# Moving 256 KB of one weight load from partitions 64-127 to partitions 0-63, and so from eight DMA engines to the other eight, in a decode kernel that streams 170 MB

## The chip, the cores and the metric

One core of one Trainium2 chip. The metric is the device time of one execution in microseconds (us), median over runs. The kernel of before took 402.03 us (401.67 to 402.33, four runs beside those of the change). All timed runs named here lie within 1.5% of the fastest run of the same kernel and count as fast.

## The reference

Two branches of a decode step for one token are added: attention over a KV cache of 65536 positions with 4 KV heads, and a small MLP "mixer". Cut to what matters:

```python
xn = layernorm(x)
# A: q = xn @ wq; softmax(q k^T) v over 65536 positions; @ wo       (the 128 MB of K and V)
# B: with S = 1 the shifted groups of h are all padding, so hs is 0 @ w2
h  = gelu(layernorm(xn) @ w1)
hs = concat(shifted quarters of h) @ w2      # w2: 1024 x 1024 bf16, 2 MB
x1 = xn + hs
h2 = gelu(layernorm(x1) @ w3) @ w4           # w3: 1024 x 3584, w4: 3584 x 1024
out = x + A + (x1 + h2)
```

The kernel still loads w2 and multiplies it, with a vector of zeros (`g_bf`). The layout of w2 in memory can therefore not change the result.

## The kernel before

All large loads are issued on one queue, in the order wq, w1, w2, w3, then K and V blocks of 8 MB (k0, v0, k1, ...), wo, and w4 in four parts. Three slots of SBUF take turns; a load is issued when its slot has been read.

```python
def rows_src(w, r0, nrow):          # partition p gets rows p*r .. p*r+r-1
    return w.rearrange("(p r) n -> p (r n)", p=P)[:, r0 * w.shape[1]:(r0 + nrow) * w.shape[1]]
kv_load(0, "s0", rows_src(A_wq, 0, 8), 8 * HQD)
kv_load(1, "w1", rows_src(B_w1, 0, 8), 8 * D, b_w1)
_dma(q_sp, chan("w2"), lambda e: e.dma_start(out=KV[:, 1, 8 * D:16 * D], in_=rows_src(B_w2, 0, 8)), writes=b_w2)
kv_load(2, "s2", rows_src(B_w3, 0, 8), 8 * F)
# ... (cut)
def proj(s, o, ncol, vec, bank, reads, c0):
    # ... for each of 8 rows j of a partition, and each column group k:
    mv = bass.AP(KV[:].tensor, s * SLOT + o + j * ncol + 4 * k, [[kvstep, P], [nper, P], [1, 4]])
    e.matmul(S_ps[...], vec[:, j:j + 1].broadcast_to([P, 32]), mv, start=(j == 0), stop=(j == KT_D - 1), ...)
# ... (cut)
proj(1, 0, D, xn2_bf, 2, b_w1 + [b_xn2], 256)
proj(1, 8 * D, D, g_bf, 3, b_w2 + [b_const], 272)     # w2 times zeros
issue(4)                                              # v0 goes into the slot of w1 and w2
# ... (cut; at the end of the kernel:)
w4_parts = [(0, 17), (17, 7), (24, 3), (27, 1)]       # rows a partition; four loads
# ... matmuls of a part start when it has landed; then one copy and the output
def Ttr(n, idx):                                      # VectorE transposes, 1024 columns each
    for ix in idx: _op(q_dve, lambda e, o=o: e.transpose(...))
```

## Time and profile before

| Reading | Value | Where it stands |
|---|---|---|
| Busy share of TensorE, VectorE | 44%, 56% | engines of the page |
| Loads' queue, share of 16 DMA engines' span | 98.4% | DMA queues |
| Last landing of w4's last load | 397.79 of 400.7 us | completion marks |
| Distance of first to last engine in that load | 3.19 us | completion marks |

Lines of the page of the kernel before: busy time of the engines, and, for 40 equal slices of the span, the granted TensorE clock in tenths, the busy share of the DMA engines in tenths and what they moved; then packets and queues.

```profile
PE 176.5 (44%) x1611; PEld 70.7 (18%) x1627; DVE 224.5 (56%) x347; ACT 25.2 (6%) x53; POOL 7.1 (2%) x30
...
PEclk9999668556655655555556656555566656555588
DMA  9999899999999999999999999999999999999994
GB/s 419 419 391 486 381 478 445 420 425 419 432 419 446 464 420 425 419 445 419 440 458 420 419 419 458 427 433 445 428 419 419 446 445 414 445 440 432 393 417 195
...
q1 hardware_dynamic: 3608, 169.87, 98.4%
q8 instruction: 13, 0.21, 0.2%
q14 instruction: 5, 0.04, 0.0%
```

The DMA engines are at least 80% busy in every slice but the last, so the kernel is bound by its loads. Two small queues carry instructions, 18 transfers in all.

The end of the chain of waits of the kernel before (start, duration, what):

```profile
369.51 0.33 SPq L534
369.84 0.05 issue
369.89 0.43 SPq L534
370.31 0.05 issue
370.37 26.78 DMA KV<-in_B_w_dram
397.14 0.04 issue
397.18 0.84 PE S_ps L543 x12
398.02 0.14 issue
398.16 0.41 PE S_ps L543 x4
398.57 0.02 issue
398.59 0.43 DVE orow L612
```

The kernel ends with a wait for parts of w4 and, in this chain, 1.9 us of work after it (397.14 to 399.02 us).

A share of busy time can't show which of 16 engines is last. The trace can: a load over 128 partitions leaves 16 completion marks. They are taken as one for each engine: the changed kernel's first load over eight partitions leaves one mark at its issue (3.27 us) and eight at its end (30.36 to 30.72 us). Here are some loads of the kernel before: time of the first mark in us of the span, then all 16 in ns after the first, sorted. (This is worked out from the trace; it is not a view of the profile.)

```
w2       31.27  0 56 67 77 88 102 112 185 195 218 244 254 264 325 393 607
k0       67.59  0 46 59 77 90 103 117 193 245 258 272 317 385 599 1179 1727
block   261.30  0 80 187 240 247 293 534 780 1473 1509 1518 1610 1660 1667 1809 2044
block   319.34  0 105 165 171 529 603 708 1529 1546 1565 1646 1697 1706 1786 1855 3052
w4 last 394.60  0 109 163 176 521 581 680 1690 1771 1807 1846 3038 3067 3083 3104 3186
```

All 16 engines move the same bytes, as far as the packets show (128, 256 or 2304 of each large size, multiples of 16, and w2's marks within 0.61 us of each other), but some fall behind in steps. The steps come from the instruction transfers: before a 16384 B one begins, its engine's marks are in the first group, after it they are 1.5 us later; a lone engine is pushed by the 8192 B ones at 60, 189 and 314 us, about 1.0 us each. (The other two 8192 B ones, at 261 and 285 us, hit other engines.) DMA records of the kernel before around the first 16 KB one (queue, start and end in ns of the span, duration, bytes):

```
1 47874 50300 2426 65536      (another engine, for comparison)
8 47899 48925 1026 16384      (instructions)
1 48920 51881 2961 65536      (the next packet of the engine that carried them)
```

That engine's packet ends at 51.88 instead of about 50.33 us: 1.55 us lost. By the end five engines are 3.0 to 3.2 us late, four 1.7 to 1.85.

### The profile page before, as it was taken

The numbers are of one execution on the slowest core, as the hardware profiler recorded it, in microseconds if no ns is written. First come the engines' busy times: TensorE is split into PE (matmuls) and PEld (weight loads), VectorE is DVE, ScalarE is ACT, GpSimd is POOL, SyncE is SP. The second block draws the span as 40 slices with busy tenths as digits, with TensorE's granted clock in tenths as the row PEclk, the third lists the DMA queues.
The fourth block names the chain that finished last, engine by engine and source line by source line (L and its number), as shares of the span: only waits on it lengthen the run. The fifth ranks groups of instructions, "written<-read, shape, count | busy, mean of one in ns | idle before, by whom it ended". The sixth has DMA issues, their size and how long they took to land.

```text
span 400.7 us, 3966 instructions
## 1 busy us (share of the span) xinstructions
PE 176.5 (44%) x1611; PEld 70.7 (18%) x1627; DVE 224.5 (56%) x347; ACT 25.2 (6%) x53; POOL 7.1 (2%) x30
## 2 busy tenths in 40 slices
PE   0034767245334513374345342643462335437664
PEld 0022435011011101121111120111121111102242
DVE  0024221985398446763985558659746685696400
ACT  1000000011001100101011001100110011010100
POOL 5000000000000000000000000000000000000000
PEclk9999668556655655555556656555566656555588
DMA  9999899999999999999999999999999999999994
GB/s 419 419 391 486 381 478 445 420 425 419 432 419 446 464 420 425 419 445 419 440 458 420 419 419 458 427 433 445 428 419 419 446 445 414 445 440 432 393 417 195
DMA packets 3770, 170.13 MB, mean 425 GB/s; under 512 B 548, under 2 KB 552, under 8 KB 808
## 3 DMA queue, kind: packets, MB, share of 16 engines
q1 hardware_dynamic: 3608, 169.87, 98.4%
q8 instruction: 13, 0.21, 0.2%
q14 instruction: 5, 0.04, 0.0%
q10 hardware_dynamic: 144, 0.00, 0.0%
HBM read 169.87 MB, written 0.00 MB: 424 GB/s over the span
## 4 chain that ended last, share of the span: by engine, by line
DMA 41%; DVE 30%; PE 23%; issue 3%; another core or an unknown queue 2%; POOL 0%; SPq 0%; ACT 0%; DVEq 0%
DMA KV<-in_A_k_cache_dram 29%; DVE KV L436 21%; PE S_ps L448 8%; DMA KV<-in_B_w_dram 7%; DMA KV<-in_A_x_dram 6%; PE OT_ps L492 5%; PE S_ps L385 3%; DVE pT_f L483 2%; PE M_ps L400 2%; DVE mrow L455 2%; PE S_ps L353 1%; PE M_ps L520 1%; DVE Yall L369 1%; PE PT_ps L479 1%
## 5 line engine op out<-in xcount | busy, mean ns | idle before, releaser
L436 DVE STREAM_TRANSPOSE KV<-KV 128x1024 f32<-128x1024 f32 x128 | 148.6, 1210 | 8.8 <-DMA KV<-in_A_k_cache_dram 8.7
L448 PE MATMUL S_ps<-KV,Yall 128*32 128x512 bf16 x512 | 60.7, 622 | 114.5 <-DVE KV L436 114.5
L492 PE MATMUL OT_ps<-KV,pT_f 128*32 128x512 bf16 x512 | 59.3, 612 | 1.3 <-PE OT_ps L492 1.3
L448 PEld LDWEIGHTS S_ps<-KV,Yall 128*32 128x32 bf16 x512 | 16.8, 125 | 148.0 <-DVE KV L436 132.2
L483 DVE STREAM_TRANSPOSE pT_f<-PT_ps 128x512 f32<-128x512 f32 x32 | 22.6, 706 | 28.2 <-PE S_ps L448 12.0
L470 ACT ACTIVATE p_sb<-S_ps,brun 128x1024 bf16<-128x1024 f32 x16 | 17.8, 1115 | 281.0 <-DVE brun L468 177.3
L455 DVE TENSOR_REDUCE mrow<-S_ps 128x1 f32<-128x1024 f32 x16 | 19.5, 1216 | 16.8 <-PE S_ps L448 16.7
L479 PE MATMUL PT_ps<-p_sb,permR 128*128 128x512 bf16 x16 | 8.8, 553 | 37.2 <-DVE pT_f L483 37.2
L492 PEld LDWEIGHTS OT_ps<-KV,pT_f 128*32 128x32 bf16 x512 | 17.1, 132 | 35.0 <-issue 33.3
L505 DVE SCALAR_TENSOR_TENSOR O_acc<-O_acc,ff,OT_ps 128x512 f32<-128x512 f32 x12 | 8.9, 744 | 23.6 <-PE OT_ps L492 23.6
L385 PE MATMUL S_ps<-KV 128*32 128x512 bf16 x88 | 12.3, 549 | 2.9 <-DVE KV L333 2.9
L458 PE MATMUL M_ps<-Rm,Lmat 128*128 128x16 bf16 x16 | 3.1, 192 | 22.6 <-DVE Rm L456 22.5
L313 DVE CAST KV<-KV 128x8 f32<-128x8 bf16 x1 | 0.2, 171 | 22.3 <-DMA KV<-in_A_x_dram 22.3
L479 PEld LDWEIGHTS PT_ps<-p_sb,permR 128*128 128x128 bf16 x32 | 3.3, 102 | 43.1 <-ACT p_sb L470 15.4
L612 DVE CAST orow<-S_ps 128x256 bf16<-128x256 f32 x1 | 0.4, 426 | 15.8 <-PE S_ps L543 15.8
L400 PE MATMUL M_ps<-ident_f,pT_f 64*128 64x2 f32 (+2 forms) x32 | 7.9, 373 | 2.3 <-DVE pT_f L393 2.3
L400 PEld LDWEIGHTS M_ps<-ident_f,pT_f 64*128 64x128 f32 (+2 forms) x32 | 7.7, 326 | 4.3 <-DVE pT_f L393 4.3
L393 DVE COPY pT_f<-S_ps 64x512 f32<-64x512 f32 (+1 forms) x3 | 2.1, 686 | 11.1 <-PE S_ps L385 11.1
L523 DVE TENSOR_TENSOR cb_R<-M_ps,maskD 32x128 f32<-32x128 f32 x4 | 1.1, 287 | 12.1 <-PE M_ps L520 12.1
L458 PEld LDWEIGHTS M_ps<-Rm,Lmat 128*128 128x128 bf16 x16 | 1.6, 102 | 34.5 <-DVE Rm L456 34.5
L338 PE MATMUL M_ps<-KV 8*128 8x8 bf16 x1 | 0.2, 161 | 16.2 <-DVE Dmat_f L337 16.2
L543 PE MATMUL S_ps<-KV,gh_bf 128*1 128x256 bf16 x112 | 4.2, 290 | 6.1 <-DMA KV<-in_B_w_dram 5.9
(82 smaller groups left out, 95.4 us busy)
## 6 DMA issues: line engine op xcount, KB each, us to landing
KV<-in_B_w_dram SPq DMA_DIRECT2D x1, 7168.0 KB, 48.1
KV<-in_B_w_dram SPq DMA_DIRECT2D x1, 4352.0 KB, 21.5
KV<-in_B_w_dram SPq DMA_DIRECT2D x2, 2048.0 KB, 28.3
KV<-in_B_w_dram SPq DMA_DIRECT2D x1, 1792.0 KB, 25.4
KV<-in_B_w_dram SPq DMA_DIRECT2D x1, 768.0 KB, 26.8
KV<-in_B_w_dram SPq DMA_DIRECT2D x1, 256.0 KB, 27.0
KV<-in_A_k_cache_dram SPq DMA_DIRECT2D x8, 38.9
KV<-in_A_v_cache_dram SPq DMA_DIRECT2D x8, 29.8
```

The lines of the kernel that those rows point to most:

```text
L385: fns.append(lambda e, j=j, k=k, mv=mv: e.matmul(S_ps[32 * (k % 4):32 * (k % 4) + 32, bank + k // 4, :], vec[:, j:j + 1].broadcast_to([P, ...
L400: fns.append(lambda e, b=b, nb=nb, c=c: e.matmul(M_ps[:, c0 + 16 * b + c:c0 + 16 * b + 4 * nb:4], pT_f[0:32 * nb, b, c:512:4], ident_f[0:3 ...
L436: _op(q_dve, lambda e, o=o: e.transpose(out=KV32[:, s, o:o + 1024], in_=KV32[:, s, o:o + 1024]), reads=[b_KV[s][4 * sub + ix]], writes=[b_ ...
L448: fns.append(lambda e, we=we, cm=cm, mv=mv: e.matmul(S_ps[32 * cm:32 * cm + 32, n % 4, :], Yall[:, h, we, :, :].rearrange("p a g -> p (a g ...
L455: _op(q_dve, lambda e: e.reduce_max(mrow[:, k:k + 1], S_ps[:, 2 * k:2 * k + 2, :].rearrange("p b c -> p (b c)"), axis=AX.X), reads=b_S[2 * ...
L458: _op(q_pe, lambda e: e.matmul(M_ps[:, 0:16], Lmat[:, :], Rm[:, k, :], start=True, stop=True), reads=[b_R[k], b_const], writes=[b_M])
L470: _op(q_act, lambda e: e.activation(p_sb[:, :, :].rearrange("p b c -> p (b c)"), S_ps[:, 2 * k:2 * k + 2, :].rearrange("p b c -> p (b c)") ...
L479: _op(q_pe, lambda e: e.matmul(PT_ps[:, :], permR[:, :], p_sb[:, n % 2, :], start=True, stop=True), reads=[b_p[n % 2], b_const], writes=[b ...
L483: _op(q_dve, lambda e: e.transpose(out=pT_f[:, n % 2, :], in_=PT_ps[:, :]), reads=[b_PT], writes=[b_pT[n % 2]])
L492: fns.append(lambda e, q=q, q4=q4: e.matmul(OT_ps[32 * q4:32 * q4 + 32, g % 2, :], pT_bf[:, n % 2, q, :, 1], KV[:, s, 8192 * sub + 512 * q ...
L505: _op(q_dve, lambda e: e.scalar_tensor_tensor(out=O_acc[:, 0:512], in0=O_acc[:, 0:512], scalar=ff[:, k:k + 1], in1=OT_ps[:, k, :], op0=ALU ...
L543: fns.append(lambda e, lhs=lhs, rhs=rhs, jj=jj: e.matmul(S_ps[32 * jj:32 * jj + 1, 0, 0:256], lhs, rhs[:, 256 * jj:256 * jj + 256], start= ...
```

## The change

w2 gets six rows on every partition by the old kind of load, and four more on partitions 0-63 by eight loads, each to eight partitions four apart. This takes 256 KB from partitions 64-127 and gives it to 0-63. In the trace after the change w3's marks stand in two groups of eight, 2.4 us apart: at the 2.42 us of a 64 KB packet that is 64 KB between them, 32 KB less for each of eight engines and 32 KB more for each of the other eight (an estimate from these two numbers). The intent is taken to be balance: the late engines would be those that lose bytes.

No record names an engine, and which engine writes which partitions of a load over 128 partitions no trace here shows. "Low" engines are here the eight that carry the loads over eight partitions, "high" ones the other eight. The recorded texts use the words in this sense, and their "half" is often one of these groups; their "lowest" and their ordinal numbers are an order that the second run of dummy loads gives (w3's marks there: one engine with one step, one with two, and so on up to two with seven, which count as the lowest).

```diff
-        _dma(q_sp, chan("w2"), lambda e: e.dma_start(out=KV[:, 1, 8 * D:16 * D], in_=rows_src(B_w2, 0, 8)), writes=b_w2)
+        NLO = 4
+        NALL = KT_D - NLO // 2
+        b_w2x = [_B() for _ in range(8)]
+        _dma(q_sp, chan("w2"), lambda e: e.dma_start(out=KV[:, 1, 8 * D:(8 + NALL) * D], in_=B_w2[0:P * NALL, :].rearrange("(p r) n -> p (r n)", p=P)), writes=b_w2)
+        for i in range(8):
+            hf, c = divmod(i, 4)
+            p0 = 32 * hf + c
+            src = bass.AP(B_w2.tensor, B_w2.offset + (P * NALL + p0 * NLO) * D, [[4 * NLO * D, 8], [1, NLO * D]])
+            _dma(q_sp, chan("w2%d" % i), lambda e, p0=p0, src=src: e.dma_start(out=KV[p0:32 * (p0 // 32) + 32:4, 1, (8 + NALL) * D:(8 + NALL + NLO) * D], in_=src), writes=[b_w2x[i]])
 ...
-        proj(1, 8 * D, D, g_bf, 3, b_w2 + [b_const], 272)
+        proj(1, 8 * D, D, g_bf, 3, b_w2 + b_w2x + [b_const], 272, NLO)
```

(`proj` runs 10 rows j instead of 8, the last four with 64 partitions, so 20 matmuls instead of 16; `g_bf` is twice as long.)

## The prediction

> **What bounds the kernel now.** In the page's slices the 16 DMA engines are 90% or more busy nearly throughout; the loads' queue has 98.4% of their span. TensorE (44%) and VectorE (56%) have slack. The chain of waits ends in a DMA wait for w4 and about 1.5 us of matmuls and copy. So the DMA engine that finishes its bytes last sets the time. All engines move the same bytes, but don't finish together: the completion marks of w2's load (16 per load) spread over 0.61 us, those of w4's last load over 3.19 us: seven engines within 0.7 us of the first, four 1.7-1.85 us late, five 3.0-3.2 us late.

> **Why.** The DMA records show 13 instruction transfers of 16384 B; each holds its engine for about 1.05 us and lengthens the next 64 KB packet from 2.42 to about 2.9 us: about 1.5 us. Following packets back to back, I find eight engines served in turn: four late ones have two, four have one. One more engine, outside these eight, takes three 8192 B instruction transfers (60, 189, 314 us) at about 1 us each and is 3 us late too. [...]

> **What the change does.** [...] Each low engine then gets 32 KB more and each high engine 32 KB less: at the traced 27.07 B/ns, +1.2 us (1.3 with smaller packets) and -1.2 us. [...] It adds four matmuls (16 took 3.4 us, so 0.85 us) and eight waits on PE in the w2 stage, and eight DMA issues (0.3-0.7 us each, under 6 us) on a queue that still has the 22 us wq load ahead. Both are hidden: v0's issue at 52 us has some 16 us before the engines run dry, k1's at 70 us likewise. w2 meets a zero vector; the result can't change.

> **On the critical path.** Only the balance. If the eight instruction engines are one half, the fifth late engine is in the other: whichever half is loaded, one engine of the +3 us class gets +1.2 us and the kernel ends later. [...] So I expect a slight loss: 403.2 us, range 401.2 to 404.3. Faster by over 2%: 0.01; within 2%: 0.98; slower by over 2%: 0.01.

> **What would show it.** Right: the spread of completion marks in w4's last load grows from 3.2 to about 4.4 us, with one or a few lone latest engines; w4's last landing about 1 us later; DMA busy unchanged in the middle; w2's 20 matmuls in about 4.2 us; k0, k1 issued about 1 us later with no idle DMA slice. Wrong: spread shrinking to about 2 us and a time near 401.

> **What would make it wrong.** [...] instruction transfers placed differently in timed runs; extra instructions bringing another transfer; eight small loads leaving an engine gap; 0.1% noise drowning it.

Passages that rested on a rule which no trace here shows are cut from it, among them which engines write which partitions. Its sum was 402.0 + 1.2 = 403.2 us: one engine of the +3 us class gets 32 KB more, 1.2 us at 27.07 B/ns. That low engines gain 32 KB and high ones lose it was a premise then; w3's marks, 2.4 us apart after the change, show it. Cut with them are two estimates on the other side of the forecast: a gain of 1.2 us if all five late engines lost bytes, and of 0.3 us if some of the +1.7 us class got them. They are no terms of the 403.2.

## The result, and the profile after

The changed kernel takes 402.82 us (402.67 to 403.12, four runs), against 402.03 us for the kernel before: a ratio of 1.0021, 95% interval 1.0004 to 1.0038. Ratios here and below are the mean time of one kernel's fast runs over that of the other's of the same rounds, so not quite the ratio of the medians quoted. It is the same within 2%, and about 0.8 us slower. All outputs are right. Run again for the experiments it was 402.87 against 402.13 us, ratio 1.0021, interval 1.0008 to 1.0033.

The same lines of the page, after:

```profile
PE 186.5 (46%) x1631; PEld 70.7 (18%) x1631; DVE 224.4 (56%) x347; ACT 25.2 (6%) x53; POOL 7.1 (2%) x30
...
PEclk9998657555755565656555556555555556655897
DMA  9999999999999999999999999999999999999994
...
q1 hardware_dynamic: 3736, 169.87, 98.3%
q8 instruction: 13, 0.21, 0.2%
q14 instruction: 5, 0.04, 0.0%
```

The bytes are the same, the DMA engines are as busy as before, and the number of instruction transfers is unchanged. The end of the chain of waits, after:

```profile
370.66 0.33 SPq L544
370.99 0.05 issue
371.04 0.44 SPq L544
371.48 0.05 issue
371.53 0.49 SPq L544
372.02 0.04 issue
372.06 26.84 DMA KV<-in_B_w_dram
398.89 0.06 issue
398.95 0.31 PE S_ps L553 x4
399.26 0.02 issue
399.28 0.42 DVE orow L622
```

The wait for w4 now ends at 398.89 us, with its last part, instead of 397.14 us with the part before the last one. The completion marks, after (as above):

```
w3       47.12  0 27 83 104 207 284 346 433 2402 2467 2524 2533 2541 2549 2569 2758
k0       66.48  0 74 104 197 275 335 432 1558 2402 2466 2524 2537 2550 2564 2758 3549
block   182.70  0 28 208 275 1477 1491 1668 1921 2341 2406 2463 2476 2490 2503 2697 3479
block   202.12  0 218 796 1421 1441 1597 1611 1865 2285 2349 2406 2417 2424 2431 2641 4403
block   240.83  0 787 1430 1450 1596 1620 1759 1873 2284 2350 2397 2417 2431 2444 2640 4402
block   260.19  0 794 1450 1474 1597 1620 1769 1874 2294 2350 2416 2430 2437 3133 4191 4413
block   280.05  0 383 925 954 1110 1125 1273 1377 1797 1862 1910 1934 1943 2636 3685 3906
block   299.38  0 363 951 971 1137 1151 1300 1405 1937 1951 1965 2563 2654 3362 3711 3925
block   318.74  0 374 960 971 1127 1151 1299 1394 1937 1951 1962 2573 2663 3372 3712 4903
w4 last 394.48  0 401 660 803 1432 1464 1481 2015 2032 2067 2157 2209 2467 2871 3223 4410
```

The change labels the engines. In w3 there are two groups of eight, 2.4 us apart: the low eight took 32 KB more, the high eight 32 KB less, 1.2 us each way as intended. Now the steps can be followed:

- The 16 KB transfer at 51.5 us hits a high engine (27 becomes 1558 in k0). So do the next five, judged by which group loses a member.
- The 8 KB transfers at 61, 191 and 317 us hit one and the same low engine. It is last in every load from k0 on (3549, then 4403, then 4903).
- The seventh 16 KB transfer, at 259.9 us, hits a low engine (2640 becomes 4191). So does the eighth, at 291.0 us (1797 becomes 3362, while the eight high marks keep their places); the ninth hits a high one again.
- The two other 8 KB transfers, at 250 and 286 us, hit two other low engines, by about 0.7 us each (3133 and 2563 are new).

So the change unloaded engines that were late, but gave 32 KB more to a low engine that was 3 us late as well. That one engine ends alone, 1.2 us behind the next, and w4's last load lands at 398.89 instead of 397.79 us.

The time grew less (0.8 us) than the landing (1.1 us). Part of this is the tail. Last matmuls of the kernel before, then of the changed one (timeline; start, duration, group):

```profile
397.18 0.81 PE L543 MATMUL S_ps<-KV,gh_bf 128*1 128x256 bf16 x12 [0.96 <-DMA KV<-in_B_w_dram]
398.16 0.38 PE L543 MATMUL S_ps<-KV,gh_bf 128*1 128x256 bf16 x4 [0.16 <-PE S_ps L543]
```

```profile
398.29 0.50 PE L553 MATMUL S_ps<-KV,gh_bf 128*1 128x256 bf16 x12 [0.95 <-DMA KV<-in_B_w_dram]
398.95 0.29 PE L553 MATMUL S_ps<-KV,gh_bf 128*1 128x256 bf16 x4 [0.16 <-DMA KV<-in_B_w_dram]
```

In the profiled run of before, twelve matmuls took 0.81 us and the last four had to wait for them although their data had landed; in the profiled run of after they took 0.50 us. The clock records of the traces show why: 0.5 of full speed from 396.76 us on in the profiled run of before, 1.0 from 395.68 to 399.09 us in that of after. For this pair the sum closes: the landing is 1.10 us later, the tail from landing to the end of the last copy 0.42 us shorter (0.81 instead of 1.23), and the profiled run took 402.67 instead of 401.99 us, 0.68 more. The tail differs from run to run (time of the profiled run less last landing: 3.8 to 4.3 us in all of those whose landing is given here; the twelve matmuls took 0.81 or 0.50 us in all whose end was read).

### The profile page after: what moved, and what is told of

Its sections match the earlier page's. It is cut to its first block, busy times and chain, and to the rows that moved or that the text cites. A ratio compares the mean times of both kernels' runs of the same rounds, so it can differ in the third digit from the quotient of the medians.

```text
span 401.4 us, 4002 instructions
## 1 busy us (share of the span) xinstructions
PE 186.5 (46%) x1631; PEld 70.7 (18%) x1631; DVE 224.4 (56%) x347; ACT 25.2 (6%) x53; POOL 7.1 (2%) x30
## 4 chain that ended last, share of the span: by engine, by line
DVE 36%; DMA 32%; PE 26%; issue 3%; ACT 2%; POOL 0%; SPq 0%; ACTq 0%; DVEq 0%
DVE KV L446 25%; DMA KV<-in_A_k_cache_dram 20%; PE S_ps L458 9%; DMA KV<-in_B_w_dram 7%; PE OT_ps L502 6%; DMA KV<-in_A_x_dram 5%; PE S_ps L395 3%; DVE pT_f L493 3%; DVE mrow L465 2%; PE PT_ps L489 2%; PE M_ps L410 2%; PE S_ps L361 2%; ACT p_sb L480 2%; PE M_ps L530 1%; DVE Yall L377 1%
## 5 line engine op out<-in xcount | busy, mean ns | idle before, releaser
L489 PE MATMUL PT_ps<-p_sb,permR 128*128 128x512 bf16 x32 | 17.8, 556 | 29.1 <-ACT p_sb L480 14.7
L395 PE MATMUL S_ps<-KV 128*32 128x512 bf16 (+1 forms) x92 | 13.0, 551 | 2.9 <-DVE KV L341 2.9
L553 PE MATMUL S_ps<-KV,gh_bf 128*1 128x256 bf16 x112 | 5.4, 355 | 7.0 <-DMA KV<-in_B_w_dram 7.0
```

The source lines that it names most:

```text
L395: fns.append(lambda e, j=j, k=k, mv=mv, pp=pp: e.matmul(S_ps[32 * (k % 4):32 * (k % 4) + 32, bank + k // 4, :], vec[0:pp, j:j + 1].broadca ...
L489: _op(q_pe, lambda e: e.matmul(PT_ps[:, :], permR[:, :], p_sb[:, n % 2, :], start=True, stop=True), reads=[b_p[n % 2], b_const], writes=[b ...
L553: fns.append(lambda e, lhs=lhs, rhs=rhs, jj=jj: e.matmul(S_ps[32 * jj:32 * jj + 1, 0, 0:256], lhs, rhs[:, 256 * jj:256 * jj + 256], start= ...
```

## The experiments

Theory (last engine): the kernel ends when the DMA engine with the most bytes and instruction transfers ends; the change added 1.2 us to such an engine, and its own instructions cost nothing. Rival (extra work): the four matmuls, the eight waits and the eight small loads cost the 0.8 us.

### The change again, as a partner for the others

> The changed kernel again, beside the others on one chip. Last-engine theory: 0.6 to 1.2 us slower than before (ratio 1.0015 to 1.003), spread of the 16 completion marks of w4's last load about 4.4 us against 3.2 us before, with one lone mark last. Extra-work theory (four matmuls, eight waits, eight small loads cost the time): the same total, so this run alone does not tell.

402.87 against 402.13 us, ratio 1.0021 (1.0008 to 1.0033). The last landing is again 398.89 us, spread 4.24 us, with one lone mark last, 1.2 us after the next. It repeats.

### Balanced bytes, all of the extra work (a flawed control)

```diff
-            src = ... [[4 * NLO * D, 8], [1, NLO * D]]      # eight partitions x four rows
+            src = ... [[16 * D, 16], [1, 2 * D]]            # sixteen partitions x two rows
-            out=KV[p0:32 * (p0 // 32) + 32:4, ...]
+            out=KV[i:P:8, ...]
```

> All added instructions of the change kept (20 matmuls on w2, eight waits, eight small loads), but each small load goes to 16 partitions with two rows, so that every engine again gets the same bytes. Last-engine theory: back to the time of before within 0.3 us (ratio 0.999 to 1.0008), spread in w4's last load about 3.2 us with five marks in the last class. Extra-work theory: stays 0.7 us or more slower than before (ratio 1.0015 or more).

It took 403.27 us, ratio 1.0028 (1.0014 to 1.0041): slower than the changed kernel, where the theory expected the time of before. The spread of the marks did go back (3.41 us, five marks in the last class), but all engines were late together: the first mark of w4's last load came at 395.85 us instead of 394.60. The small packets explain it: the 4096 B packets took 267 ns in the median and 159 at least, a mean of 255, and w3's packets 2172 ns in the mean instead of 2118. Eight of each per engine make 8 x 96 + 8 x 54 = 1200 ns, an estimate from these means, against 1250 ns observed. Why packets to these partitions (every eighth) were slower is not shown. The run is no test of the rival. It shows that the way in which the loads are cut can cost more than the change itself.

### The extra rows on partitions 64-127

```diff
-            p0 = 32 * hf + c
+            p0 = 64 + 32 * hf + c
```

(with the source and the matmuls moved to match)

> The extra rows go to partitions 64-127 instead of 0-63, still by loads of eight rows. If a load of eight rows runs on the lowest eight engines whatever partitions it writes: as the changed kernel, w4's last landing near 398.9 us of the span, one lone mark last at about 4.4 us. If the engine follows the partition: the high eight engines get the extra 32 KB, the low eight lose it, four marks (those with two 16 KB instruction transfers) last, the spread about 5 to 5.5 us (3.05 + 1.2 over low engines that are now 1.2 us earlier), the time likewise about 1.2 us over before. Extra-work theory: as the changed kernel in both.

It took 405.85 us, ratio 1.0091 (1.0077 to 1.0104), more than either side expected. The marks settle which engines did it: in w3 again eight are late by 2.26 us or more, and the engine with the three 8 KB instruction transfers is among the eight, while the first 16 KB one hits the other eight, as in the changed kernel. So, as far as these marks tell, the loads over eight partitions ran on the same eight engines for partitions 64-127 as for 0-63. But the first mark of w3 came at 49.80 us instead of 47.12: the high engines lost time too. The 8192 B packets took 643 ns in the median; in the changed kernel, where they go to partitions 0-63, they took 309.

### Dummy loads over 2 to 8 rows

```diff
+        for k in range(2, 9):
+            p0 = k * (k - 1) // 2                     # second run: (0, 1, 2, 3, 32, 33, 34)[k - 2]
+            src = bass.AP(B_w2.tensor, B_w2.offset, [[32 * D, k], [1, 16 * D]])
+            _dma(... out=KV[p0:p0 + k, 1, 16 * D:32 * D] ...)   # second run: every fourth partition
```

> Kernel before plus seven dummy loads over 2, 3, ... 8 rows of 32 KB each (1.21 us per engine). If a load over k rows runs on the lowest k engines: in w3's completion marks, eight engines without a step, and one each later by 1.2, 2.4, 3.6, 4.8, 6.0, 7.2 us and two by 8.5 us, beside the base spread of 0.6 us. The instruction transfers of 16 KB then should all fall on the eight without a step, and the lone engine with three 8 KB ones on one of the steps, which tells its number. Total about 8.5 us longer, more if the lone engine is a low number (up to 11).

418.63 us (one run). Eight marks of w3 stayed together and eight moved, but by 4.0, 4.6, 5.1, 5.4, 7.6, 8.0, 8.9 and 11.3 us: the 32 KB packets took 2.36 us in the median instead of 1.21. The steps can't be read. These loads write neighbouring partitions; that this made them slow was a guess. So I ran it again with every fourth partition:

> Dummy loads over 2, 3, ... 8 rows again, now to every fourth partition, so that each should write at full rate (1.21 us for 32 KB). In w3's completion marks: eight without a step; eight at about 1.2, 2.4, 3.6, 4.8, 6.0, 7.3 and twice 8.5 us. The engine with three 8 KB instruction transfers (the first near 62 us) is the one whose mark moves about 1 us later from w3 to the next load, or that is already 1 us off its step if its w3 mark comes after that: the step tells its number among the low eight.

408.17 us (one run). The 32 KB packets took 1.21 us, and the marks now are a ladder:

```
w3  48.33  0 39 85 131 141 151 200 210 1346 2363 3566 4792 6109 7665 8403 8814
k0  67.68  0 48 85 124 137 151 205 218 1356 3566 3924 4792 7087 7674 8393 8814
```

A load over k rows ran on k engines, among them all those of the smaller loads: one engine with one step, one with two, and so on. Between the two loads 6109 became 7087 and 2363 became 3924. The engine five steps up (the fourth from the ladder's end) took the 8 KB transfer at 61 us; the engine two steps up (the seventh from the end) took the 16 KB one at 52.6 us. So the engines of the 16 KB transfers are not one half of the sixteen: this one is low, and the changed kernel shows two low ones. The second surprise is that here a low one was hit by the first of the thirteen transfers, in the changed kernel none before the seventh.

### The extra work alone, and the matmuls alone

```diff
 # work only: kernel before, w2 whole, plus eight loads of 512 B a row and four repeated matmuls
+            src = bass.AP(B_w2.tensor, B_w2.offset + p0 * 4 * D, [[16 * D, 8], [1, 256]])
-        proj(1, 8 * D, D, g_bf, 3, b_w2 + [b_const], 272)
+        proj(1, 8 * D, D, g_bf, 3, b_w2 + b_w2x + [b_const], 272, 2)
 # matmuls only: no small loads, no further waits
+        proj(1, 8 * D, D, g_bf, 3, b_w2 + [b_const], 272, 2)
```

> Kernel before with the change's extra work and without its shift: w2 stays at eight rows on all partitions, four matmuls are repeated (20 in all), and eight loads over eight rows carry 512 B a row only (about 31 ns of an engine each). Last-engine theory: as before, 0 to 0.35 us slower (eight packets and marks on the low engines), spread of the marks of w4's last load 3.2 to 3.5 us. Extra-work theory: 0.7 us or more slower. This replaces the balanced run[...].

402.50 against 401.94 us, ratio 1.0012 (1.0000 to 1.0025): between the two, and not decisive. The last landing was 398.30 us, 0.5 us later than before, where 0.3 us had been put down to the packets and marks.

> Kernel before with only the four repeated matmuls in w2's stage (20 instead of 16), no small loads and no further waits: the half of the work-only run that puts no byte on any DMA engine. Last-engine theory: the time of before, ratio 0.9993 to 1.0007; v0 and k1 are issued 0.5 to 1 us later and w4's last landing stays near 397.8 us of the span. Extra-work theory, if the matmuls were what cost in the work-only run (402.50 against 401.94): about 0.5 us slower, ratio 1.001 or more.

401.93 against 402.11 us, ratio 0.9997 (0.9983 to 1.0010). The matmuls cost nothing that these runs can resolve. The last landing was 398.10 us, though, where about 397.8 was expected: it can vary by 0.3 us between kernels of the same time, so the 0.5 us of the work-only run is less sure than it looks. The 20 matmuls ran later and longer, as the timeline of this kernel shows (w2's matmuls, and v0's issue right after):

```profile
48.45 4.04 PE L386 MATMUL S_ps<-KV 128*32 128x512 bf16 x20
52.59 0.33 SPq L265 DMA_DIRECT2D KV<-in_A_v_cache_dram  x1
```

In the kernel before:

```profile
48.41 3.46 PE L385 MATMUL S_ps<-KV 128*32 128x512 bf16 x16
51.97 0.33 SPq L265 DMA_DIRECT2D KV<-in_A_v_cache_dram  x1
```

v0 is issued 0.6 us later, while the engines have k0 to move until 67 us. So what the work-only run lost, if it lost anything, came with the small loads and their waits.

### Fewer VectorE instructions

```diff
-            for ix in idx:                       # Ttr: one transpose of 1024 columns each
-                _op(q_dve, ... KV32[:, s, o:o + 1024] ...)
+            w = 1024 * len(idx)                  # one transpose for neighbours
+            _op(q_dve, ... KV32[:, s, o:o + w] ...)
 # and one Yall product for each head instead of four
```

> Kernel before with the same merged VectorE instructions. Last-engine theory: the four engines with two 16 KB instruction transfers still end at about 3.1 us, so the time stays within 0.3 us of before (ratio 0.9993 to 1.0005), and four instead of five marks are in the last class. If the fewer VectorE instructions themselves made the kernel faster: about 1 us faster here too.

401.91 against 401.94 us, ratio 0.9995 (0.9983 to 1.0008). Four marks instead of five in the last class, and the same time: VectorE's instructions are not the limit, and taking one late engine out of five saves nothing.

> The changed kernel with 76 fewer VectorE instructions (four transposes merged into one where nothing stands between them, sixteen Yall products into four), so that VectorE's third instruction transfer (now at 317 us, at its 310th of 382 recorded instructions) is not needed. Last-engine theory, with the last engine's lateness caused by VectorE's instruction transfers: that engine is 2 instead of 3 us late before the shift, the spread in w4's last load falls from 4.4 to about 3.3 us and the time by about 1 us against the changed kernel, to 401.6 to 402.1. If those 8 KB transfers are not VectorE's, or do not set the end: as the changed kernel, 402.8.

402.27 us (401.69 to 403.22), ratio 1.0007 (0.9993 to 1.0020). The cause of the 8 KB transfers is confirmed: four are left instead of five; the low engine is hit at 61.6 and 239 us (3624 becomes 4575 there) and not a third time. But the time fell by half of what was expected, and the five runs lie 1.5 us apart, wider than any other kernel here. In the profiled run (402.96 us) a low engine was hit by the first of the 16 KB transfers and again by the ninth, and was last; the eighth hit the other low one (the 3860 below):

```
w3       47.06  0 83 169 189 208 257 475 504 2423 2587 2693 2714 2817 2840 2900 4223
block   318.60  0 510 1026 1222 1253 1310 1520 1908 2081 2344 2714 2902 2909 3579 3860 4335
block   337.95  0 511 1037 1224 1245 1312 1512 1928 2092 2346 2716 2903 2916 3862 4356 5122
w4 last 393.85  0 505 1308 1507 1897 2076 2340 2577 2700 2767 2785 2879 2892 3841 4321 5109
```

> The changed kernel with fewer VectorE instructions again, whose five timed runs lay 1.5 us apart (401.69 to 403.22). Theory: the round of 16 KB transfers over eight engines (seven high, one low) starts at another engine in another execution. Where the low one is met once (12 of 13 transfers on others, found at the second to eighth or sixth place), the last mark is about 3.3 us and the time near 401.8; where it is met twice (first to fifth place), it is last at about 5 us and the time near 403. So: again a spread of over 1 us, and the place of the low engine's transfer in the profile goes with that run's time. If the place is the first again in this profile, and the times are not spread, this falls.

402.32 us (402.01 to 403.28), ratio 1.0014 (1.0002 to 1.0027): again over 1 us apart. The profiled run was a fast one (402.03 us), and here the two low engines were hit by the sixth (a mark of about 2590 became 4137 in the load that landed from 241 us) and the seventh (2597 became 4128 in that from 279 us), so once each; the last landing was 398.24 instead of 398.96 us. The place goes with the time in these two executions, as expected. The spread did not fall to 3.3 us, though: it was 4.31, the low engine of the 8 KB transfers still being last. Two profiles are few; that the start of the round explains all of the scatter is not shown.

### More to three engines only

```diff
-        (six rows on all, eight loads of four rows to eight partitions)
+        # seven rows on all; 120 rows by four loads of ten rows to partitions i, i+4, i+8; 8 rows by one load
+            src = bass.AP(B_w2.tensor, B_w2.offset + (7 * P + 10 * i) * D, [[40 * D, 3], [1, 10 * D]])
+            _dma(... out=KV[i:12:4, 1, 15 * D:25 * D] ...)
-        proj(..., 272, NLO)
+        proj(..., 272, (P,) * 7 + (12,) * 10 + (8,))      # 36 matmuls
```

> Seven rows of w2 on all partitions, 120 rows by four loads over three rows (so on the lowest three engines, which the graded run shows without the repeated late transfers: the lone 8 KB engine took five steps there and is the fourth, the low engine with a 16 KB one took two steps and is the seventh), the last 8 rows by one load; 36 matmuls on w2 instead of 16. The three engines get about 2.4 us more, the other thirteen 0.6 us less. Last-engine theory: late engines 3.1 - 0.6 = 2.5 us, the three 2.4 us over their 0.1 to 0.7: the spread of marks in w4's last load is 2.5 to 3.1 us and the time 0 to 0.5 us below before (ratio 0.9987 to 1.0003), about 1 us below the changed kernel, although there is more extra work on TensorE. Extra-work theory: 0.7 us or more slower than before (ratio 1.0015 or more).

402.20 against 401.93 us, ratio 1.0004 (0.9990 to 1.0017). With 36 matmuls on w2 and five small loads it is not slower than before by the 0.7 us of the rival, and three marks of w3 (3392, 3482, 3574) stand apart from thirteen within 0.4 us. It gains nothing either. The three engines lie 3.4 us behind the others, not 3.0 (2.4 + 0.6), and one of them was hit by an 8 KB instruction transfer at 288 us (its mark went from 3489 to 4162), so that it was last at the end. I had used up the room that the other engines' lateness left. No version that beats the kernel before was found.

### Twice the shift

```diff
-        NLO = 4
+        NLO = 8
```

> The change doubled: four rows on all partitions and eight extra on 0-63 by the same eight loads; each low engine 64 KB (2.4 us) over before, each high one 2.4 us below. Last-engine theory: 1.2 us over the changed kernel, 1.8 to 2.6 us over before (ratio 1.0045 to 1.0065), spread of marks in w4's last load 5.5 us or more plus what the high engines gained (up to 7 us). Extra-work theory (eight loads as before, four more matmuls): at most 0.8 us over the changed kernel and no larger spread.

404.21 against 401.93 us, ratio 1.0059 (1.0046 to 1.0072): 2.3 us over before, as the last-engine theory put it, with the same number of small loads and four more matmuls, which cost nothing in the matmuls-only run. So the 1.5 us between the doubled and the changed kernel can't be put down to more loads or matmuls. The end of the chain of waits of this kernel:

```profile
373.17 26.68 DMA KV<-in_B_w_dram
399.85 0.04 issue
399.89 0.84 PE S_ps L553 x12
400.73 0.14 issue
400.87 0.41 PE S_ps L553 x4
401.28 0.02 issue
401.30 0.42 DVE orow L622
```

w4's last landing was 400.50 us, 2.7 us after that of before. The spread in that load was 4.1 us, not the 5.5 to 7 us expected: in w3 it was 5.4, but the first mark of the load that lands from 282 us came 21.1 us after the first of the one before it, where 19.4 is the pace, and the last mark kept the pace of 19.4. So the engines that were ahead lost 1.7 us there. The trace shows a load that was issued late: v's issue stands at 260.28 us (257.50 in the kernel before), the first engine had ended the block before it at 260.91, and the first packet of the new load starts at 261.46; the first packets of the engines ahead then took up to 3.73 us instead of 2.42. The issue was 2.8 us later than in the kernel before, and so was the last mark of the block landing from 242 us (246.84 against 243.98), which the late engine sets. That the one caused the other fits, but was not tested. In the changed kernel the first engine lost 0.5 us in the same stretch (19.86 us from 260.19 to 280.05), the last one nothing.

## Why the prediction was right or wrong

- **The bound.** Right: the DMA engines are busy in all slices but the last in both kernels, and the end is set by the last mark of w4.
- **What the change moves.** Right: 2.4 us between the groups of eight in w3, that is 1.2 us each way.
- **The step that decides: "whichever half is loaded, one engine of the +3 us class gets +1.2 us".** Right: the engine with three 8 KB transfers is low, and ends alone. Measured: spread 3.19 to 4.41 us ("to about 4.4"), last landing 1.1 us later ("about 1 us later").
- **"If the eight instruction engines are one half".** Wrong as a premise: six are high and two low (one is the engine two steps up the ladder, if it is the same one), in all four profiles where the round could be followed (the changed kernel twice, the same with merged VectorE instructions twice). The conclusion, for the half loaded here, needs only that the engine of the three 8 KB transfers is low. The prediction had this from the wrong premise alone, so that part was luck; had that engine been a high one, the change could have gained some 0.4 us (an estimate: 1.5 + 1.2 us for a low engine with one 16 KB transfer, against 3.1 before). In the two executions profiled here of the changed kernel the two low ones had one 16 KB transfer each.
- **The time.** 402.8 measured, 403.2 predicted. The 1.2 us of shift was not all seen, 0.8 us was. In the profiled pair the tail's granted clock accounts for the gap between landing and time (0.42 us); the start of the round can differ as well. How the two share the difference in the timed runs is open, since those have no marks.
- **Extra work hidden.** Right for the matmuls (0.9997 with them alone). Their size was off: 20 took 3.62 us in the changed kernel, not 4.2. k1 was issued 2.0 us later (72.35 against 70.31 us), not 1, and no idle DMA slice followed. For the small loads it is not settled: the work-only run leaves 0 to 1.0 us.
- **Not foreseen at all:** that a small load's rate changes with its destination (8 KB packets to every fourth partition took 309 ns in the half 0-63, 643 ns in 64-127; 32 KB ones 1.21 us to every fourth partition, 2.36 us to neighbouring ones). The change's own destinations had the 309 ns.

## What to carry to other kernels

When the DMA engines are busy throughout, look at when each of the sixteen ends, not at their mean: unequal completion marks show where time may be left, and what pushes single engines. Before moving bytes between engines, find out who every late engine is; unloading most of them gains nothing while one of them gets more. Measure the packets of a load over a few partitions: with other destination partitions they took about twice as long here (643 against 309 ns, 2.36 against 1.21 us).

## What the traces show of the instruction transfers

- In this kernel, bound by its loads, each 16 KB transfer took about 1.5 us from one DMA engine (a 16384 B packet of the loads took 0.61 us; why the transfer costs more is not shown), and four engines with two of them each ended 3 us late.
- The 16384 B ones here are put down to TensorE from their spacing (some 250 of its recorded instructions; no run tested it); VectorE's came as 8192 B, some 120 recorded instructions apart (at its 69th, 186th and 310th), and cost about 1.0 us each. One of them went away with VectorE's merged instructions.
- Those put down to TensorE went round eight engines, six high and two low, starting at another one in another execution; the three of VectorE in the kernel before, and in the changed one, all went to one engine, in the latter a low one; in the ladder the first went to the engine five steps up. The engines that fell behind in these runs did so in steps that coincide with instruction transfers.
